# Attention fused with a soft mixture of experts: block pairs first in even steps, four pages with the first keys, at most two pages in a block, and the last values' places given back sooner

## The chip, the cores and the metric

The kernel runs on one core of one Trainium2 chip. The metric is the device time of one execution in microseconds (us); the time of a kernel is the median over several executions. Engines are named as in the profile: PE is TensorE's matrix multiply and PEld its weight load, DVE is VectorE, ACT is ScalarE, POOL is GpSimd and SP is SyncE, which here only issues transfers.

## What is computed

The reference has two stages. The first is attention for 8 batches and 8 heads with head size 64: 512 local positions, which see a window of 32 positions to each side and all 32 global keys, and 32 global positions, which see everything. The second is a soft mixture of 8 experts with 4 slots each: all 4352 rows of the attention's output are mixed into 32 slots by a softmax over the rows, each expert runs a two-layer network on its 4 slots, and each row gets its output from the slots by a softmax over the slots.

```python
k_all = np.concatenate([k_g, k_l], axis=2); v_all = np.concatenate([v_g, v_l], axis=2)
out_g = np.matmul(sm(scale * np.matmul(q_g, k_all.transpose(0, 1, 3, 2))), v_all)
s_ll = np.where(np.abs(pos[:, None] - pos[None, :]) <= 32, scale * q_l @ k_l.T, -1e9)
out_l = np.matmul(sm(np.concatenate([scale * q_l @ k_g.T, s_ll], axis=-1)), v_all)
x = concatenate([out_g, out_l], axis=2), heads side by side: rows of 512
logits = x @ phi
slot_input = softmax(logits, over rows).T @ x
slot_out[e] = np.maximum(slot_input[e] @ w1[e], 0.0) @ w2[e]
return softmax(logits, over slots) @ slot_out
```

(`sm` is a softmax with 1e-9 added to its sum; matrix shapes are shortened.) All inputs are float32. w1 and w2 together are 32 MB, q, k and v as laid out for loading some 30 MB, the output 8.9 MB.

## The kernel before, in words

**Steps.** Two heads of one batch make a step; there are 32, numbered s = 0 to 31, with batch b = s // 4, k = s % 4, and unit u = s // 2 for the global rows. The loop of line 573 runs steps 0 to 29; steps 30 and 31 and the rest are written out from line 665 on. A step holds, on PE: `scores(s)` (line 233, the 16 blocks of 32 queries against their windows of keys, 64 weight rows by 32 columns, then the masks as small products); `pv(s - 1)` (line 271, the weighted values of the step before); in odd steps `global_scores(u)` and `global_pv(u - 1)`; at k = 2 the logits of the batch before (`Dispatch.logits`, line 411), at k < 2 half of the slot sums of the batch before that (`Dispatch.sums`, line 473); in even steps transposes of x (`turn_x`, line 393) and of the global weights; and at the end `turn_exp(s)` (line 258), which transposes the shifted scores and has ACT take the exponentials. DVE takes the maxima (`top`, L251), subtracts them (`shift`, L256), divides (`norm`, L280 to L288) and keeps the running maxima and sums of the slots (L423 `Dispatch.top`, L486 `Dispatch.add`).

**pv.** It works in 16 blocks of 32 queries. 12 of them are single (32 columns of weights), and the pairs (0, 1) and (14, 15) share a window and are done with 64 columns. `GROUPS` (lines 61 and 62) lists the singles and then the two pairs; `pv` goes through it in parts of 4, 4, 4 and 2, each part for head e = 0 and then e = 1. Each float32 product is two passes on PE, so a pv is 48 passes of singles and 8 of pairs. The values stand in three tiles with shifted rows: `v` as loaded, `va` and `vb`, which POOL builds from it in `make_v` (line 195): five copies make va (L201 to L205), two make vb (L207, L208). v has 5 places (tag "v"), va 2, vb 1. A pair reads v or va, never vb; among the singles, blocks 3, 6, 9 and 12 read vb, blocks 2, 5, 8, 11 (and 13) read va.

**Loads.** All loads go through SP's queue in program order (`dma`, line 176). PE's instructions are counted in `step_count`; when the count passes a multiple of 255.22, a block begins: `pump()` (line 536) issues the block's loads, and the first of them waits for the matmul at which the block began. In a block with room for keys, pump issues one `kq` (keys and queries of a step, 592 KB) and, if a place is free, one `v` (325 KB), otherwise a page; in a block with room for a v alone, the v and a page; in any other block two pages, or three when all v are issued or when the count of pages is behind 2.5 per such block (`blocks`, `PACE`, lines 534 and 553 to 556). A page is 512 KB of w1 or w2 (`load_page`, line 499); there are 64, in the order in which the experts use them. 33 (`NWA`) have places of their own from the start.

**The tail.** After the steps, `go(n)` (line 680) issues n loads that wait for the last matmul traced: pages into own places while there are any, then whatever stands in `ready`; when ready is empty, go does nothing. The last 31 pages take places of tiles that are no longer needed: four places of kq (`borrow`, line 690), one in the area of the scores and global weights (`a2`, by the pool `wA`), six in the area of the values (`at`, by the pool `wC`), four in two places of xh (`rows_slot`, line 787), and 16 in places of pages that the first product has used (`quad`, line 910). Before the areas are free, the transposed x of the last batch (`xTm`, made in `turn_both`, line 741, and `turn_global`, line 748) is put into the five places with tag "v". Then come the logits (line 797), the slot sums, `first_product` (line 917) over pages 0 to 31, `second_product` (line 962) over pages 32 to 63 for the left half of the columns (h = 0) and for the right (h = 1), and `combine` (line 988), which makes the rows of the output from the slots and has SP store them: the left halves of the batches between the parts of the second product of h = 1, and the right halves after it.

Of the kernel before, what the change touches and what calls it, by code (L numbers as in the profile page):

```python
# [7 lines left out]
F32 = mybir.dt.float32  # L8
# [10 lines left out]
P = 128  # L19
# [39 lines left out]


SINGLE = tuple((c, 1) for c in (2, 3, 12, 13, *range(4, 12)))
GROUPS = SINGLE + ((0, 2), (14, 2))

# [12 lines left out]
def kernel(  # L76
# [194 lines left out]
    def pv(s):  # L271
        for i, j in ((0, 4), (4, 8), (8, 12), (12, 14)):
            for e in range(2):
                for c, n in GROUPS[i:j]:
                    t, qd = c // 4, c % 4
                    v, m = values(s, c)
                    q = slice(32 * qd, 32 * (qd + n))
                    mm(bV[q, t, VD * e:VD * e + VD], Ps[s][:, e, t, q], v[:, m, e, :], start=True, stop=True)
# [254 lines left out]
    free = {"kq": -1, "v": -1}  # L533
    blocks, PACE = [0], 2.5

    def pump():


        if due["kq"] < NST and due["kq"] - 4 <= free["kq"]:
            load_kq(due["kq"])  # L540
            due["kq"] += 1
            if due["v"] < NST and due["v"] - 5 <= free["v"]:
                load_v(due["v"])
                due["v"] += 1
            elif npage[0] < NWA:
                load_slot(npage[0])
        elif due["v"] < due["kq"] and due["v"] - 5 <= free["v"]:
            load_v(due["v"])
            due["v"] += 1
            if npage[0] < NWA:  # L550
                load_slot(npage[0])
        else:
            blocks[0] += 1
            for _ in range(2 + (due["v"] == NST or npage[0] + 2 < PACE * blocks[0])):
                if npage[0] < NWA:
                    load_slot(npage[0])
        gate[0] = None
# [113 lines left out]
    def pump():  # L671
# [6 lines left out]
        gate[0] = None  # L678

    def go(n):  # L680

        for _ in range(n):
            gate[0] = last[0]
            if npage[0] < NWA:
                load_slot(npage[0])
            elif ready:
                ready.pop(0)()
        gate[0] = None
# [71 lines left out]
    def both(hc, n=4):  # L760
        xTm[hc] = at.tile([P, n, NT if hc != "g" else SG], F32, tag="v", name="xTm", bufs=5)

    turns["s"] = turns["v"] = 0
    both((1, 0))
    turn_both(1, "s")
    pv(s)
    go(1)
    both("g")
    turn_global((0, 1), nc.scalar.copy)
    both((2, 0))  # L770
    turn_both(2, "s")
    d6.totals()
    both((3, 0), 2)
    both((3, 2), 2)
    norm(s)
# [4 lines left out]
    pa6 = ptile("s", 512)  # L780
    p_a2.close()
    fin = ctx.enter_context(tc.tile_pool(name="fin", bufs=1, reuse_waits="tile"))
    wA = ctx.enter_context(tc.tile_pool(name="wA", bufs=1, reuse_waits="tile"))
    new = lambda pool, tag, i: lambda: load_page(pool.tile([P, 1024], F32, tag=f"{tag}{i}", name=f"w{npage[0]}", bufs=1))
    ready.append(new(wA, "wA", 0))

# [5 lines left out]

    p_at.close()
    wC = ctx.enter_context(tc.tile_pool(name="wC", bufs=1, side="right", reuse_waits="tile"))
    ready += [new(wC, "wC", i) for i in range(NWC)]
    go(3)
    for hc in ("g", 0, 1, 2, 3):
        c = slice(P, NT) if hc == "g" else slice(0, P) if hc == 0 else slice(0, NT)
        for t in range(4):
# [6 lines left out]
            mm(pl[32 * t:32 * t + 32, c], phisb[:, 0 if hc == "g" else hc, :], x, start=(hc == "g"), stop=(hc == 3))  # L806
    go(1)
    d6.sums(pa6, 0, 512)
# [179 lines left out]
    def combine(h, b, whole=True):  # L988
# [12 lines left out]
        else:  # L1001
            os = [wC.tile([P, 4, 256], F32, tag=f"wC{b - 2}", name=f"ob{h}_{b}", bufs=1)]
        n = 4 if b < B else 2
# [125 lines left out]
```

## Time and profile before

| | us |
|---|---|
| median of 3 runs | 265.3 |
| lowest and highest run | 264.77, 267.85 |
| profiled execution, its time | 266.62 |
| its span, first to last instruction | 264.8 |
| mean granted clock of TensorE in it | 0.98 |

A line of groups gives the source line, engine, operation, the tiles as out<-in with their shapes, how often, the busy time and mean duration, and the engine's idle time ahead with what ended it. A line of waits reads: who waited <- for whom: us in total, times, longest. The view in order of time gives start, duration, engine, line, operation, tiles, shape and count; instructions of the same kind that follow each other are merged, and a shape such as 128*32 is the weight's rows and columns. "SPq" rows are transfers being issued, not their data. Line numbers are those of the kernel before, and a line can be that of a helper: L164 is every matmul, L167 every transpose and L177 every load.

### The profile page before, as it was taken

How to read it: one execution, taken by the hardware profiler on the slowest of the kernel's cores; microseconds unless marked ns; L12 is line 12 of the kernel's file. 1: busy time of each engine (PE TensorE's matmuls, PEld its weight loads, DVE VectorE, ACT ScalarE, POOL GpSimd, SP SyncE). 2: the span in 40 equal slices, each digit the busy share in tenths (PEclk: the TensorE clock that was granted, in tenths of full speed). 3: DMA queues.
4: the chain of work that ended last, by engine and by line, in shares of the span. 5: the costliest groups of instructions: out<-in, count | busy, mean ns of one | idle time of the engine just before them, and what ended most of it. 6: DMA issues, size and time to landing. Idle time of an engine off the chain costs nothing.

```text
span 264.8 us, 14386 instructions
## 1 busy us (share of the span) xinstructions
PE 244.8 (92%) x6438; PEld 177.6 (67%) x6438; DVE 174.1 (66%) x373; ACT 100.7 (38%) x225; POOL 127.2 (48%) x292
## 2 busy tenths in 40 slices
PE   8699999999999999999999999999999999999860
PEld 5578778778777777787777878777784334644430
DVE  0686677877978788777778796978775233333650
ACT  0334534434454443354544545443454003133330
POOL 0785775738685756676474738675740000000000
PEclk9799999999999999999999999999999999999995
DMA  7957587877676787868776877669699999999998
GB/s 223 321 179 244 206 259 246 256 273 233 223 237 219 243 268 254 245 244 285 230 245 231 262 271 238 213 188 336 217 368 322 386 415 411 408 408 373 341 342 286
DMA packets 27870, 73.82 MB, mean 279 GB/s; under 512 B 2464, under 2 KB 11040, under 8 KB 27808
## 3 DMA queue, kind: packets, MB, share of 16 engines
q1 hardware_dynamic: 27808, 72.90, 80.1%
q8 instruction: 50, 0.82, 1.2%
q14 instruction: 12, 0.10, 0.1%
HBM read 63.98 MB, written 8.91 MB: 275 GB/s over the span
## 4 chain that ended last, share of the span: by engine, by line
PE 73%; DVE 15%; ACT 3%; DMA 2%; issue 2%; SPq 1%; DVEq 0%; POOL 0%
PE bM L164 14%; PE bT L167 13%; PE pair L164 12%; PE bV L164 12%; PE bS L164 11%; PE one L164 4%; DVE sp L256 3%; DVE mx L251 3%; PE bV L167 3%; DMA kq<-in_kq_dram 2%; DVE xh L288 2%; PE bM L167 2%; ACT xT L408 1%; DVE ob L1009 1%; DVE lv L370 1%
## 5 line engine op out<-in xcount | busy, mean ns | idle before, releaser
L267 ACT ACTIVATE sp<-bT 128x512 f32<-128x512 f32 x64 | 34.8, 595 | 60.8 <-PE bT L167 56.8
L251 DVE TENSOR_REDUCE mx<-bS 128x8 f32<-128x1024 f32 x31 | 37.9, 1221 | 18.8 <-PE bS L164 18.6
L164 PE MATMUL bV<-va,sp 128*32 128x65 f32 (+1 forms) x768 | 41.8, 224 | 1.1 <-DVE xh L288 0.7
L256 DVE TENSOR_TENSOR sp<-bS,mx 128x1024 f32<-128x1024 f32 x31 | 38.0, 1224 | 4.8 <-PE bV L164 1.3
L164 PEld LDWEIGHTS bV<-va,sp 128*32 128x32 f32 (+1 forms) x768 | 33.6, 114 | 9.2 <-issue 7.2
L167 PE MATMUL bT<-con,sp 128*128 128x128 f32 x256 | 34.7, 279 | 2.4 <-DVE sp L256 2.4
L164 PE MATMUL bS<-kq 64*32 64x128 f32 x1984 | 36.3, 274 | 0.0
L201 POOL COPY va<-v 128x520 f32<-128x520 f32 x32 | 19.9, 622 | 33.7 <-DMA v<-in_vS_dram 30.1
L167 PEld LDWEIGHTS bT<-con,sp 128*128 128x128 f32 x256 | 28.4, 142 | 7.5 <-DVE sp L256 3.6
L164 PE MATMUL bV<-v,sp 128*32 128x65 f32 (+1 forms) x512 | 32.5, 223 | 0.4 <-issue 0.4
L164 PEld LDWEIGHTS bS<-kq 64*32 64x32 f32 x1984 | 27.7, 105 | 5.3 <-issue 5.1
L164 PE MATMUL bV<-vb,sp 128*32 128x65 f32 x512 | 28.6, 223 | 0.2 <-POOL vb L208 0.2
L164 PEld LDWEIGHTS bV<-v,sp 128*32 128x32 f32 (+1 forms) x512 | 25.7, 116 | 3.4 <-issue 0.5
L350 POOL COPY xg<-og 32x64 f32<-32x64 f32 x64 | 14.8, 231 | 25.5 <-DVE og L344 16.4
L288 DVE TENSOR_TENSOR xh<-bV,r 128x512 f32<-128x512 f32 x32 | 22.1, 691 | 3.8 <-PE bM L164 2.9
L164 PEld LDWEIGHTS bV<-vb,sp 128*32 128x32 f32 x512 | 23.2, 109 | 0.4 <-POOL vb L208 0.3
L164 PE MATMUL bM<-kq 64*32 64x128 f32 (+3 forms) x256 | 20.1, 343 | 2.8 <-DMA kq<-in_kq_dram 2.5
L207 POOL COPY vb<-v 64x520 f32<-64x520 f32 x32 | 19.7, 616 | 4.4 <-PE bV L164 2.7
L202 POOL COPY va<-v 32x520 f32<-32x520 f32 x32 | 19.6, 612 | 2.0
L208 POOL COPY vb<-v 64x520 f32<-64x520 f32 x32 | 19.6, 612 | 1.7
L1009 DVE COPY ob<-pair 128x512 f32<-128x512 f32 x19 | 12.4, 687 | 10.4 <-PE pair L164 10.3
L164 PEld LDWEIGHTS bM<-kq 128*64 128x64 f32 (+1 forms) x256 | 13.6, 141 | 6.3 <-DMA kq<-in_kq_dram 2.8
(195 smaller groups left out, 411.9 us busy)
## 6 DMA issues: line engine op xcount, KB each, us to landing
w<-in_w_dram SPq DMA_DIRECT2D x64, 512.0 KB, 6.6
kq<-in_kq_dram SPq DMA_DIRECT2D x31, 592.0 KB, 4.2
v<-in_vS_dram SPq DMA_DIRECT2D x32, 325.0 KB, 4.7
out_dram<-ob SPq DMA_DIRECT2D x14, 512.0 KB, 4.4
out_dram<-ob SPq DMA_DIRECT2D x4, 256.0 KB, 4.5
kq<-in_kq_dram SPq DMA_DIRECT2D x2, 296.0 KB, 3.1
out_dram<-ob SPq DMA_DIRECT2D x4, 128.0 KB, 3.5
mks<-in_mk_dram SPq DMA_DIRECT2D x1, 176.0 KB, 3.6
```

Of the source, the lines that this page charges most:

```text
L164: return step_count(4 if rhs.dtype == F32 else 2, nc.tensor.matmul(o, lhsT, rhs, **kw))
L167: return step_count(2, nc.tensor.transpose(o, a, i))
L201: cp(va[:, 0:4], v[:, 0:4])
L202: cp(va[0:32, 0:4], v[0:32, 1:5])
L207: cp(vb[64:128], v[64:128, 0:4])
L208: cp(vb[0:64], v[0:64, 1:5])
L251: nc.vector.reduce_max(mxs[s], bank(s).rearrange("p e t k -> p (e t) k"), axis=AX.X)
L256: nc.vector.tensor_tensor(sps[s], bank(s).rearrange("p e t k -> p (e t) k"), bc(mxs[s], P), ALU.subtract)
L267: nc.scalar.activation(Ps[s][:, e], pt, AF.Exp, scale=SCALE)
L288: nc.vector.tensor_tensor(xhs[b][:, hc].rearrange("p t (e d) -> p t e d", e=2), o[:, :, :, 0:D], bc(r, D), ALU.mult)
L350: engines[j](xgs[b // 4][p0:p0 + 32, 256 * g + D * j:256 * g + D * j + D], ogs[u][32 * j:32 * j + 32])
L1009: copies[turn[0] % 2](os[i] if not whole else os[0][:, 2 * i:2 * i + 2, :], pcs[i])
```

## The change

Four things are edited.

1. `pv` takes the pairs of blocks first when s is odd, which is the pv that runs in an even step, and last when s is even, as before. `GROUPS` becomes `SINGLE` and `PAIRS`.
2. `pump` adds a page to a block with kq and v as long as fewer than 9 kq have been issued, and a block without kq or v gets two pages, or three only when all v are issued; `blocks` and `PACE` are gone.
3. `go` remembers in `owed` what it could not issue for want of an entry in `ready` and issues it at a later go.
4. In the tail, the transposed x of head pair 1 and of the global rows share one place with tag "va" instead of two with tag "v"; the other three keep places with tag "v". The pools `a2` and `at` are closed right after pv(31). `wC` becomes six pools of one page each, opened in the reverse order, the fourth and sixth are filled first, the other four after the logits; the fifth is 1072 wide instead of 1024, of which the page uses 1024.

```diff
--- before.py
+++ after.py
@@ -58,8 +58,9 @@
 
 
 
+
 SINGLE = tuple((c, 1) for c in (2, 3, 12, 13, *range(4, 12)))
-GROUPS = SINGLE + ((0, 2), (14, 2))
+PAIRS = ((0, 2), (14, 2))
 
 
 def block_window(c):
@@ -269,9 +270,10 @@
     xhs = {}
 
     def pv(s):
-        for i, j in ((0, 4), (4, 8), (8, 12), (12, 14)):
+        parts = [SINGLE[i:i + 4] for i in range(0, 12, 4)]
+        for part in parts + [PAIRS] if s % 2 == 0 else [PAIRS] + parts:
             for e in range(2):
-                for c, n in GROUPS[i:j]:
+                for c, n in part:
                     t, qd = c // 4, c % 4
                     v, m = values(s, c)
                     q = slice(32 * qd, 32 * (qd + n))
@@ -531,7 +533,6 @@
 
     due = {"kq": 3, "v": 2}
     free = {"kq": -1, "v": -1}
-    blocks, PACE = [0], 2.5
 
     def pump():
 
@@ -539,10 +540,11 @@
         if due["kq"] < NST and due["kq"] - 4 <= free["kq"]:
             load_kq(due["kq"])
             due["kq"] += 1
-            if due["v"] < NST and due["v"] - 5 <= free["v"]:
+            v = due["v"] < NST and due["v"] - 5 <= free["v"]
+            if v:
                 load_v(due["v"])
                 due["v"] += 1
-            elif npage[0] < NWA:
+            if npage[0] < NWA and (not v or due["kq"] < 9):
                 load_slot(npage[0])
         elif due["v"] < due["kq"] and due["v"] - 5 <= free["v"]:
             load_v(due["v"])
@@ -550,8 +552,7 @@
             if npage[0] < NWA:
                 load_slot(npage[0])
         else:
-            blocks[0] += 1
-            for _ in range(2 + (due["v"] == NST or npage[0] + 2 < PACE * blocks[0])):
+            for _ in range(2 + (due["v"] == NST)):
                 if npage[0] < NWA:
                     load_slot(npage[0])
         gate[0] = None
@@ -677,13 +678,17 @@
                 ready.pop(0)()
         gate[0] = None
 
+    owed = [0]
+
     def go(n):
 
-        for _ in range(n):
+        owed[0] += n
+        while owed[0] and (npage[0] < NWA or ready):
+            owed[0] -= 1
             gate[0] = last[0]
             if npage[0] < NWA:
                 load_slot(npage[0])
-            elif ready:
+            else:
                 ready.pop(0)()
         gate[0] = None
 
@@ -758,31 +763,38 @@
                     copy(xTm[hc, t0][:, :, P:NT], p[:, t0:t1])
 
     def both(hc, n=4):
-        xTm[hc] = at.tile([P, n, NT if hc != "g" else SG], F32, tag="v", name="xTm", bufs=5)
+        xTm[hc] = at.tile([P, n, NT], F32, tag="v", name="xTm", bufs=5)
 
     turns["s"] = turns["v"] = 0
-    both((1, 0))
+    x1 = at.tile([P, 6, P], F32, tag="va", name="xT1").rearrange("p a b -> p (a b)")
+    xTm[1, 0] = x1[:, 0:4 * NT].rearrange("p (t k) -> p t k", k=NT)
+    xTm["g"] = x1[:, 4 * NT:4 * NT + P].rearrange("p (t k) -> p t k", k=SG)
+    both((2, 0))
+    both((3, 0), 2)
+    both((3, 2), 2)
     turn_both(1, "s")
     pv(s)
+    p_a2.close()
+    fin = ctx.enter_context(tc.tile_pool(name="fin", bufs=1, reuse_waits="tile"))
+    wA = ctx.enter_context(tc.tile_pool(name="wA", bufs=1, reuse_waits="tile"))
+    new = lambda pool, tag, i: lambda: load_page(pool.tile([P, 1024], F32, tag=f"{tag}{i}", name=f"w{npage[0]}", bufs=1))
+    ready.append(new(wA, "wA", 0))
+
+    p_at.close()
+    wC = [ctx.enter_context(tc.tile_pool(name=f"wC{i}", bufs=1, side="right", reuse_waits="tile"))
+          for i in reversed(range(NWC))][::-1]
+    ready += [new(wC[i], "wC", i) for i in (3, 5)]
     go(1)
-    both("g")
     turn_global((0, 1), nc.scalar.copy)
-    both((2, 0))
+    go(2)
     turn_both(2, "s")
     d6.totals()
-    both((3, 0), 2)
-    both((3, 2), 2)
     norm(s)
     turn_global((2, 3), nc.vector.tensor_copy)
     turn_both(3, "v", 0, 2)
     turn_both(3, "s", 2, 4, nc.vector.tensor_copy)
     pl = banks["m"][1][:, 0:NT]
     pa6 = ptile("s", 512)
-    p_a2.close()
-    fin = ctx.enter_context(tc.tile_pool(name="fin", bufs=1, reuse_waits="tile"))
-    wA = ctx.enter_context(tc.tile_pool(name="wA", bufs=1, reuse_waits="tile"))
-    new = lambda pool, tag, i: lambda: load_page(pool.tile([P, 1024], F32, tag=f"{tag}{i}", name=f"w{npage[0]}", bufs=1))
-    ready.append(new(wA, "wA", 0))
 
     def rows_slot():
 
@@ -790,10 +802,6 @@
         load_page(t[:, 0])
         load_page(t[:, 1])
 
-    p_at.close()
-    wC = ctx.enter_context(tc.tile_pool(name="wC", bufs=1, side="right", reuse_waits="tile"))
-    ready += [new(wC, "wC", i) for i in range(NWC)]
-    go(3)
     for hc in ("g", 0, 1, 2, 3):
         c = slice(P, NT) if hc == "g" else slice(0, P) if hc == 0 else slice(0, NT)
         for t in range(4):
@@ -804,7 +812,10 @@
             else:
                 x = xTm[hc, t // 2 * 2 if hc == 3 else 0][:, t % 2 if hc == 3 else t, :]
             mm(pl[32 * t:32 * t + 32, c], phisb[:, 0 if hc == "g" else hc, :], x, start=(hc == "g"), stop=(hc == 3))
-    go(1)
+
+    wide = lambda: load_page(wC[4].tile([P, 1072], F32, tag="wC4", name=f"w{npage[0]}", bufs=1)[:, 0:1024])
+    ready += [*(new(wC[i], "wC", i) for i in range(3)), wide]
+    go(3)
     d6.sums(pa6, 0, 512)
     go(1)
     ready.append(rows_slot)
@@ -999,7 +1010,7 @@
         elif b < 2:
             os = [kqp.tile([P, 4, 256], F32, tag="kq", name=f"ob{h}_{b}", bufs=4)]
         else:
-            os = [wC.tile([P, 4, 256], F32, tag=f"wC{b - 2}", name=f"ob{h}_{b}", bufs=1)]
+            os = [wC[b - 2].tile([P, 4, 256], F32, tag=f"wC{b - 2}", name=f"ob{h}_{b}", bufs=1)]
         n = 4 if b < B else 2
         pcs = [ptile("c", 2, 512)[:, :, 0:256] for _ in range(n // 2)]
         for t in range(n):
```

## The prediction

> **What bounds the kernel now.** I read the page first, for the engines' shares and the chain of work that ended last; then the table by stretches, to split the attention steps (up to about 196 us) from the experts' stage; then TensorE's own waits in these two parts.
>
> ```profile
> PE 244.8 (92%) x6438; PEld 177.6 (67%) x6438; DVE 174.1 (66%) x373; ACT 100.7 (38%) x225; POOL 127.2 (48%) x292
> ...
> PE 73%; DVE 15%; ACT 3%; DMA 2%; issue 2%; SPq 1%; DVEq 0%; POOL 0%
> ```
>
> In the next view the columns behind each stretch are the busy times of PE, PEld, DVE, ACT and POOL, the granted clock, DMA's share and its GB/s.
>
> ```profile
> 10.00:20.00 10.00, 9.58 (x263) 7.71 (x248) 7.49 (x11) 3.66 (x7) 8.11 (x17) 0.90 0.65 205
> 20.00:40.00 20.00, 19.38 (x659) 15.59 (x659) 13.34 (x25) 8.44 (x16) 13.83 (x33) 1.00 0.75 239
> 40.00:60.00 20.00, 19.99 (x601) 16.16 (x600) 15.53 (x32) 8.19 (x19) 11.34 (x26) 1.00 0.76 253
> 196.00:206.00 10.00, 9.60 (x200) 5.78 (x188) 5.17 (x22) 3.76 (x12) 1.05 (x5) 1.00 0.94 349
> 206.00:216.00 10.00, 9.77 (x94) 3.32 (x90) 3.11 (x11) 0.00 (x0) 0.00 (x0) 1.00 1.02 404
> ```
>
> TensorE carries 73% of the chain and is busy nearly all of every stretch; DMA is busy three quarters of the time in the steps and without a pause in the experts' stage (1.02). So the steps are TensorE's, while two suspects stand in the experts' stage. The waits tell them apart. From 6 to 196 us TensorE's list holds one transfer, at the start, and from 196 us to the end none; the longest rows of the two lists:
>
> ```profile
> PE bM L164 <- DMA kq<-in_kq_dram: 2.5, 1, 2.5
> PE bT L167 <- DVE sp L256: 2.4, 6, 0.7
> ```
>
> ```profile
> PE pair L164 <- ACT sa L981: 0.5, 1, 0.5
> ```
>
> No matmul of the experts waits for a page. What ends last are the outputs, which need the experts' last products; SP issues the last four from 256.23 us:
>
> ```profile
> 184.55 45.38 SPq L177 DMA_DIRECT2D w<-in_w_dram  x36
> ...
> 256.23 3.49 SPq L1014 DMA_DIRECT2D out_dram<-ob  x4
> ```
>
> The 36 pages are issued over 45.38 us, 1.26 us each: my price of a page where DMA is full. The end is set by TensorE's chain to the last products, plus the output drain behind it.
>
> **Part 1, pairs of blocks first in even steps.** pv(s - 1) runs in step s, so the order changes for odd s - 1: in even steps, in pv(29) of the tail and in pv(31). No matmul is added; what changes is which shapes are neighbours. TensorE's order of time around pv(15), in step 16 (start, duration; the shape is weight rows*columns):
>
> ```profile
> 98.00 0.42 PE L164 MATMUL bS<-mks 64*32 64x384 bf16 x8
> 98.35 0.24 PE L164 MATMUL bV<-va,sp 128*32 128x65 f32 x1
> ...
> 98.97 0.22 PE L164 MATMUL bV<-vb,sp 128*32 128x65 f32 x1
> 99.01 0.22 PE L164 MATMUL bV<-v,sp 128*32 128x65 f32 x1
> ...
> 99.03 0.22 PE L164 MATMUL bV<-vb,sp 128*32 128x65 f32 x1
> 99.18 0.27 PE L164 MATMUL bV<-v,sp 128*64 128x65 f32 x1
> ...
> 99.41 0.22 PE L164 MATMUL bV<-va,sp 128*64 128x65 f32 x1
> 99.56 0.64 PE L164 MATMUL bM<-xh,d 128*32 128x256 f32 x8
> 100.13 0.66 PE L167 MATMUL bT<-con,xh 128*128 128x128 f32 x4
> ```
>
> From the last single (99.03) to the first pair (99.18) it is 0.15 us, from the last pair (99.41) to the first sum (99.56) again 0.15; where the shape stays 128*32, four more start 0.04 after the last of the four before (98.97 to 99.01). A change of shape costs 0.11 beyond that cadence. Now there are four changes in such a step: masks to singles, singles to pairs, pairs to sums (or logits), these to transposes. Pairs first leave three: masks to pairs, pairs to singles, and behind the singles' sums the transposes. That saves 0.11. The sums also start up quicker: after a change they take 0.57 (99.56 to 100.13), without one, in the next step, 0.55:
>
> ```profile
> 106.58 0.62 PE L164 MATMUL bM<-xh,d 128*32 128x256 f32 x8
> 107.13 0.44 PE L167 MATMUL bT<-con,sp 128*128 128x128 f32 x2
> ```
>
> That makes 0.13 us in each even step with sums or logits right behind pv: by the code steps 6 to 28 (logits at k = 2 from b = 1, sums at k = 0 from b = 2), 12 steps. In steps 2 and 4, in step 30 and after pv(31) transposes follow, and the number of changes stays. In odd steps pairs stay last, ahead of the 128*64 global scores: nothing changes.
>
> Does VectorE let the saving through? Its subtraction for the next transposes ends at 101.06 in step 16, and they begin at 101.17, so there at most 0.11 can reach TensorE; I take half, 0.05, for this step and for one more like it.
>
> ```profile
> 99.83 1.23 DVE L256 TENSOR_TENSOR sp<-bS,mx 128x1024 f32<-128x1024 f32 x1
> ```
>
> ```profile
> 101.17 0.28 PE L167 MATMUL bT<-con,sp 128*128 128x128 f32 x1
> ```
>
> But VectorE itself idles in even steps for ScalarE's xT copy, which comes from transposes right behind pv and the sums; its list of waits:
>
> ```profile
> DVE acc L486 <- ACT xT L408: 5.4, 6, 1.8
> DVE bm L423 <- ACT xT L408: 4.4, 4, 1.6
> ```
>
> So VectorE's work for the odd step behind it moves up with TensorE, and the rest passes: 10 x 0.13 + 2 x 0.05 = 1.4 us.
>
> Unseen is masks straight to pairs (64*32 to 128*64). Every change above starts the next matmul 0.07 before the end of the one ahead (98.00 + 0.42 against 98.35, 99.03 + 0.22 against 99.18, 99.41 + 0.22 against 99.56, 99.56 + 0.64 against 100.13), whatever the shapes; so I take masks to pairs like masks to singles, no difference. The bounds are a change that is free, 0.11 less, and one that costs double, 0.11 more: 1.5 us either way over the 14 pv's behind masks (steps 4 to 30). The Trainium skill (TensorEngine Tiling (Array Packing), Key Properties) says that a change of tiling mode drains TensorE; by that rule it costs what is in flight, the masks in both orders, and the sum stays; no row here shows this pair of modes.
>
> **Part 1b, late values.** Pairs need v and va, not vb, so pairs first postpone the first read of vb by 0.23 for the pairs (99.18 to 99.41) and 0.15 for the change: 0.38 us. Twice vb was late, in pv(9) and pv(25):
>
> ```profile
> 61.87 0.30 PE L164 MATMUL bV<-va,sp 128*32 128x65 f32 x2
> 62.13 0.25 PE L164 MATMUL bV<-vb,sp 128*32 128x65 f32 x2
> ```
>
> ```profile
> 160.16 0.30 PE L164 MATMUL bV<-va,sp 128*32 128x65 f32 x2
> 160.61 0.25 PE L164 MATMUL bV<-vb,sp 128*32 128x65 f32 x2 [0.15 <-POOL vb L208]
> ```
>
> The stalls are 0.26 and 0.45 us. The first is covered whole; of the second 0.38 is, and part 2 should take the other 0.07. I count 0.7. In return pv gives vb back up to 0.4 us later in even steps. POOL is behind five va copies then; should it come early, POOL would wait 0.4, and TensorE only if vb were the last to be ready.
>
> **Part 2, the page rhythm.** I ran the rule of pump() by hand with the counts of the code. kq and v keep blocks and order. The first blocks of kq3, kq4, kq6 and kq7 get a page each: four more by step 5. The blocks of three in steps 15, 19, 23 and 29 become blocks of two: four fewer. Before step 30's first block both versions have issued 28 pages, which the trace confirms for the kernel before (64 less the 36 above). So this brings nothing into the tail earlier. Four pages cost 4 x 1.26 = 5.0 us of DMA early, where the stretches above leave 0.35 x 10 + 0.25 x 20 + 0.24 x 20 = 13.3 idle. On SP a page is one more issue behind v; the next kq and v in the queue wait for their own block anyway. The bounds are 0 and one page, 1.26 us, of delay to the v that is already latest, v9 in pv(9); I take 0.
>
> The block of three in step 23 is the one that hurt: v25 was issued behind it, POOL waited 3.99 us for it, and vb came late in pv(25).
>
> ```profile
> 145.22 2.39 SPq L177 DMA_DIRECT2D w<-in_w_dram  x3
> ...
> 150.06 0.38 SPq L177 DMA_DIRECT2D v<-in_vS_dram  x1
> ```
>
> ```profile
> 156.77 0.62 POOL L201 COPY va<-v 128x520 f32<-128x520 f32 x1 [3.99 <-DMA v<-in_vS_dram]
> ```
>
> A page less ahead of v25 is up to 1.26 us; 0.07 of it is needed.
>
> **Part 3, places of the last values.** The last batch's transposed x moves from five "v" places to three and one "va" place, the pools close before norm(31), and pages go into the new places sooner: two after pv(31), one after the next transposes, four behind the logits; go() remembers what it could not issue. Compute order is the same. SP's new wait is for pv(31) to leave sp. All later pages queue behind it, and matmuls use those only in the second product, after all 32 pages of the first. What the stream can gain is DMA's idle share here, 0.06 of the 10 us from 196: 0.6 us. Since no expert matmul waits for a page, I count 0 at the end; if that cover were gone, 0.6.
>
> **Sum.** The profiled execution has a span of 264.8 us in a time of 266.62, 1.8 around it. 264.8 - 1.4 - 0.7 = 262.7, with 1.8 264.5. That execution lies 1.3 above the median of the runs, 265.3; on the median it is 265.3 - 2.1 = **263.2 us**.
>
> **Rivals.** (a) *DMA sets the end.* The full stretch speaks for it, the waits without a page against it. Then part 3 adds its 0.6: 262.6. The Trainium skill (Perfetto Trace Analysis, Identifying the Most-Contended Engine) will not take matmul busy time as TensorE's measure and looks at weight loads; they fill 3.32 of 10 us at 206 to 216, beside a full DMA, so by that rule the stage is DMA's and this rival's time holds. (b) *VectorE absorbs the saved changes.* For it: six waits of TensorE for sp. Against: VectorE's waits for xT. Only the 0.7 is left: 264.6. (c) *Early pages push v9.* It lands 1.26 later and pv(9) waits 0.26 + 1.26 - 0.38 = 1.1, where I forecast none: 264.3. (d) *Slower: masks to pairs is dear.* Place: the 14 pv's behind masks. It decides from 2.1 / 14 = 0.15 on top of masks to singles, more than a whole change (0.11), against the four changes that all look alike; at 0.25 it is 14 x 0.25 = 3.5 less the 2.1: 266.7. (e) *The change doesn't do what it says*: the stalls move and the changes of shape cost what they did, 265.3.
>
> **How the numbers follow.** Forecast 0.53, (a) 0.13, (b) 0.14, (c) 0.08, (d) 0.06, (e) 0.04, something unseen and faster 0.02. The likeliest's own range is 261.7 to 264.7, by the masks' bounds of 1.5. All cases but (d) lie in 261.7 to 265.3; the runs of one kernel here go from 264.77 to 267.85, so I take 261.3 to 265.9, which leaves (d) and the unseen out. Two per cent is 5.3 us, about what a measurement of this kernel can tell from no change: below 260.0 only the unseen (0.02) comes, above 270.6 only (d) well beyond its price (0.02).
>
> **What would show it.** Right: pv to sums 0.04 apart in steps 6 to 28; masks to first pair like masks to first single now, 0.35 from the first mask; no wait for vb in pv(9) and pv(25); 28 pages before step 30; TensorE's end 2 us earlier with the drain behind it as long as now. Wrong: masks to pairs 0.15 dearer, new waits for vb in steps 5 to 10, pages in TensorE's waits after 206 us, or an end that moves without TensorE's.

## The result, and the profile after

The changed kernel is slower by about 1%: 268.6 us median of 6 runs (268.07 to 271.26) against 266.48 us of the kernel before (264.77 to 272.06, 6 runs), a ratio of 1.0106 with a 95% interval of 1.0059 to 1.0152. On another chip (e9_after_again below) it was 1.0066 (1.0028 to 1.0104). The forecast was 2 us less. The profiled execution took 268.07 us with a span of 266.3; the one of before 266.62 with 264.8. Line numbers are one higher than before ahead of `pv` and more behind it. Ratios leave out executions more than 1.5% above a kernel's fastest, and the profiled executions of e1_pairs, e6_no_early and e13_pairs_pump are such, so of them only the ratios are used, and one list of stalls.

Busy time and the chain of waits that ended last, from the page of the changed kernel:

```profile
PE 242.6 (91%) x6438; PEld 176.4 (66%) x6438; DVE 174.7 (66%) x373; ACT 100.4 (38%) x225; POOL 126.8 (48%) x292
...
PE 74%; DVE 14%; issue 3%; ACT 2%; DMA 2%; SPq 1%; DVEq 1%
```

TensorE is busy 2.2 us less than before, and "issue", time in which it waits for nothing that the profile shows, has grown from 2% to 3% of the chain. The same five stretches as before (busy PE, PEld, DVE, ACT, POOL, granted clock, DMA's share, GB/s):

```profile
10.00:20.00 10.00, 8.81 (x255) 7.03 (x254) 6.77 (x11) 4.17 (x9) 7.79 (x16) 1.00 0.80 272
20.00:40.00 20.00, 17.31 (x589) 13.78 (x569) 12.57 (x23) 7.67 (x14) 13.63 (x33) 1.00 0.90 303
40.00:60.00 20.00, 20.00 (x644) 16.22 (x640) 15.60 (x30) 7.96 (x18) 11.54 (x26) 1.00 0.76 244
196.00:206.00 10.00, 9.57 (x208) 5.97 (x208) 5.28 (x21) 4.20 (x13) 1.40 (x6) 1.00 1.01 393
206.00:216.00 10.00, 9.77 (x92) 3.41 (x95) 2.79 (x10) 0.00 (x0) 0.00 (x0) 1.00 1.03 413
```

From 20 to 40 us DMA is at 0.90 where it was at 0.75, and TensorE is busy 17.31 us where it was 19.38: 2 us are lost where the early pages load. TensorE's waits from 6 to 196 us:

```profile
PE bT L168 <- DVE sp L257: 3.0, 6, 0.9
PE bS L165 <- issue: 2.7, 2, 1.9
PE bM L165 <- DMA kq<-in_kq_dram: 1.7, 1, 1.7
```

The longest wait with no releaser before was 0.4 us; now one of 1.9 us stands there. In TensorE's order of time it is in step 6, between two halves of the same mask products, which have the same operands:

```profile
37.52 0.40 PE L165 MATMUL bS<-mks 64*32 64x384 bf16 x4
39.85 0.34 PE L165 MATMUL bS<-mks 64*32 64x384 bf16 x4 [1.93 <-issue]
```

What was on its way in that time is seen in SP's list, in which the third row is three pages in two blocks, one of them the early page beside kq7 and v6:

```profile
31.08 0.33 SPq L178 DMA_DIRECT2D kq<-in_kq_dram  x1
31.50 1.16 SPq L178 DMA_DIRECT2D v<-in_vS_dram  x1
32.72 2.91 SPq L178 DMA_DIRECT2D w<-in_w_dram  x3
```

And the queues show a passenger that the prediction did not look at. The page's third part has 50 transfers of 16 KB on a queue of their own, named instruction: the engines' code, loaded while the kernel runs.

```profile
q1 hardware_dynamic: 27808, 72.90, 79.3%
q8 instruction: 50, 0.82, 1.2%
```

In the steps one comes every 4 us or so. Between 32.4 and 37.5 us, 5.1 us, there is none, with the engines 92% full of loads (packets, MB, share):

```profile
q1 hardware_dynamic: 428, 1.46, 92.2%
q14 instruction: 1, 0.01, 0.4%
```

In the kernel before, the stretch with the same loads of kq7 and v6, from 31.6 to 36.4 us, is 62% full and has one such transfer at its beginning; the next one starts at 36.52:

```profile
q1 hardware_dynamic: 284, 0.94, 61.7%
q8 instruction: 1, 0.02, 1.8%
```

In the changed kernel it comes in the next stretch, from 37.5 to 38.6 us: one packet, 5.6% of 16 engines for 1.1 us, that is 0.99 us long.

```profile
q8 instruction: 1, 0.02, 5.6%
```

The trace has it from 37.58 to 38.57, and TensorE goes on 1.28 us later, at 39.85. This is a rule and not a single case: in both kernels every idle time of TensorE of 0.12 us or more between 9 and 206 us for which the profile names no releaser ends 1.2 to 1.9 us after the end of a q8 transfer. Over the fourteen profiles of the table further down it holds for 93 of 95 such times, where by chance about one in six would fall into these 0.7 us (the transfers in the steps are 4.3 us apart on average). I call these stalls *late code*. That q8 carries TensorE's own code is inferred: its 6438 products and 6438 weight loads over 50 transfers are 257 instructions a transfer, and the kernel's blocks of loads are 255.22 counted instructions long, so code and loads come nearly in step. Late code comes to 1.4 us in the kernel before and 4.3 in the changed one; between 30 and 45 us alone to 0.26 and 2.34.

The other loss is behind the last product. TensorE's last products are copied out 0.6 us later than before, but the end is 1.45 later. The last two copies, of before and then of the changed kernel:

```profile
255.90 1.29 DVE L1009 COPY ob<-pair 128x512 f32<-128x512 f32 x2 [0.80 <-PE pair L164]
```

```profile
256.49 1.29 DVE L1020 COPY ob<-pair 128x512 f32<-128x512 f32 x2 [0.80 <-PE pair L165]
```

From the end of these (257.18 and 257.78) to the end of the span it is 7.6 us and 8.5 us. I call this the drain. The rate at which outputs leave, in a stretch ahead of it and one in it, again before and then after:

```profile
253.18:255.18 2.00, 2.00 (x18) 1.10 (x18) 1.29 (x2) 1.16 (x3) 0.00 (x0) 1.00 1.08 383
258.18:261.18 3.00, 0.00 (x0) 0.00 (x0) 0.00 (x0) 0.00 (x0) 0.00 (x0) 0.50 1.09 385
```

```profile
253.78:255.78 2.00, 2.00 (x18) 1.05 (x17) 1.29 (x2) 1.16 (x3) 0.00 (x0) 1.00 1.01 343
258.78:261.78 3.00, 0.00 (x0) 0.00 (x0) 0.00 (x0) 0.00 (x0) 0.00 (x0) 0.78 1.03 348
```

DMA is full in all four, yet it moves 383 and 385 GB/s before and 343 and 348 after. These outputs are mostly the right halves of batches 2 to 7, which leave from the wC places that part 3 moved.

The difference between the two profiled executions adds up so: the changed one was 1.05 us ahead at step 4 (its first keys came sooner, which is not of the change); step 6 turns this into 0.90 behind; the rest of the steps and the experts win 0.30 back; the drain loses 0.85: 1.45 in all.

### The profile page after: what moved, and what is told of

It reads as the page before. It is cut to its first block, busy times and chain, and to the rows that moved or that the text cites. A ratio compares the mean times of both kernels' runs of the same rounds, so it can differ in the third digit from the quotient of the medians.

```text
span 266.3 us, 14383 instructions
## 1 busy us (share of the span) xinstructions
PE 242.6 (91%) x6438; PEld 176.4 (66%) x6438; DVE 174.7 (66%) x373; ACT 100.4 (38%) x225; POOL 126.8 (48%) x292
## 4 chain that ended last, share of the span: by engine, by line
PE 74%; DVE 14%; issue 3%; ACT 2%; DMA 2%; SPq 1%; DVEq 1%
PE bT L168 14%; PE bM L165 13%; PE bS L165 12%; PE pair L165 12%; PE bV L165 12%; PE one L165 4%; DVE sp L257 3%; DVE mx L252 3%; PE bV L168 3%; PE bM L168 2%; DMA kq<-in_kq_dram 2%; DVE xh L290 2%; DVE ob L1020 1%; ACT xT L410 1%; DVE cm L370 1%
## 5 line engine op out<-in xcount | busy, mean ns | idle before, releaser
L165 PE MATMUL bV<-v,sp 128*32 128x65 f32 (+1 forms) x512 | 34.1, 224 | 0.6 <-ACT sp L268 0.4
L165 PE MATMUL bM<-kq 64*32 64x128 f32 (+3 forms) x256 | 19.2, 308 | 2.1 <-DMA kq<-in_kq_dram 1.7
L165 PEld LDWEIGHTS bM<-kq 128*64 128x64 f32 (+1 forms) x256 | 13.0, 129 | 5.5 <-DMA kq<-in_kq_dram 2.1
```

What stands on the lines that cost most here:

```text
L165: return step_count(4 if rhs.dtype == F32 else 2, nc.tensor.matmul(o, lhsT, rhs, **kw))
```

## The experiments

The theory: part 1 gives what was forecast; the early pages of part 2 stand in front of TensorE's code and make it late; part 3 puts the outputs in places that are read more slowly. Rivals: the pairs cost elsewhere; part 2 is neutral; the drain is long because of the order of transfers; the stalls come by chance.

### The parts alone

e1_pairs: the kernel before with the edit of `pv` alone.

```diff
-        for i, j in ((0, 4), (4, 8), (8, 12), (12, 14)):
+        parts = [SINGLE[i:i + 4] for i in range(0, 12, 4)]
+        for part in parts + [PAIRS] if s % 2 == 0 else [PAIRS] + parts:
             for e in range(2):
-                for c, n in GROUPS[i:j]:
+                for c, n in part:
```

> The kernel before with part 1 alone: pairs first in even steps. Theory of late code: the change as a whole came out slower because TensorE stands still in the middle of products that wait for nothing the profile shows, each time shortly after the end of a 16 KB transfer of the queue q8 instruction, and the early pages delay these transfers. It expects here what part 1 and 1b of the prediction priced, 2.1 us less than the kernel before (ratio 0.992), pv(9) and pv(25) without their stalls, and no stall of over 1 us in step 6. Rival, the pairs cost elsewhere: VectorE's small operations in steps 22 and 23 (0.4 us later there in the changed kernel) and pv(31) (0.18 longer) come from the new order; then this kernel gains at most 1.0 us (ratio 0.996 or more).

Measured: 0.9917 (0.9873 to 0.9961), 2.2 us less, which is what was forecast for the pairs and more than the 1.0 us that the rival allowed. The size is less sure than the interval says: only six of the twelve runs enter the ratio, and the medians of all runs, 267.29 us against 267.10 of the kernel before beside them, show no gain. e11_pairs_tail_wide below, which has the pairs too, is 1.8 us less than the kernel before.

e2_pump: the kernel before with the edit of `pump` alone.

```diff
-            elif npage[0] < NWA:
+            if npage[0] < NWA and (not v or due["kq"] < 9):
...
-            for _ in range(2 + (due["v"] == NST or npage[0] + 2 < PACE * blocks[0])):
+            for _ in range(2 + (due["v"] == NST)):
```

> The kernel before with part 2 alone: four early pages, never three in a block. Theory of late code: slower by 2 to 3.5 us (ratio 1.008 to 1.013), with TensorE idle for about 2 us without a releaser between 33 and 42 us, after a q8 instruction transfer that started 5 us or more behind the one before. Rival, part 2 is neutral as forecast: within 0.7 us of the kernel before, the stall of 0.45 us in pv(25) gone.

Measured: 1.0060 (1.0023 to 1.0098), 1.6 us more: slower, by somewhat less than expected. TensorE's order of time from 30 to 45 us has the loss in two pieces, at the same two places of the program as in the changed kernel:

```profile
34.48 0.87 PE L164 MATMUL bM<-kq 128*64 128x256 f32 x8 [1.17 <-issue]
39.30 0.34 PE L164 MATMUL bS<-mks 64*32 64x384 bf16 x4 [0.55 <-issue]
```

e3_tail: the kernel before with part 3 alone (go, the places of xTm, the pools; the diff of the change from go on).

> The kernel before with part 3 alone: places of the last values given back sooner, wC in six pools. Theory of late code: no change (ratio 0.998 to 1.002). Rival, the drain: the outputs of the last batches leave from new places and their packets of 1024 bytes take 48 to 50 ns where they took 46 to 47; then the last product ends as before and the end is 0.9 us later (ratio 1.003).

Measured: 1.0010 (0.9974 to 1.0046). The ratio can't tell 0 from 0.9 us, but the drain can: 8.3 us, where e2_pump had 7.8. So the long drain comes with part 3.

e4_pairs_tail: the changed kernel with the old page rhythm.

```diff
-            if npage[0] < NWA and (not v or due["kq"] < 9):
+            elif npage[0] < NWA:
...
-            for _ in range(2 + (due["v"] == NST)):
+            blocks[0] += 1
+            for _ in range(2 + (due["v"] == NST or npage[0] + 2 < PACE * blocks[0])):
```

> The changed kernel with the page rhythm of the kernel before, so parts 1 and 3 without part 2. Theory of late code: 2.1 us faster than the kernel before (ratio 0.992), like the pairs alone. Rival drain: 1.2 us faster (0.9955), 0.9 lost after the last product. Rival pairs cost elsewhere: no faster than 1.0 us (0.996).

Measured: 1.0009 (0.9971 to 1.0048), slower than any of the three said, with a drain of 8.3 and only 0.8 us of late code in the profiled execution. By itself this was a riddle; e11_pairs_tail_wide below takes it up again.

e13_pairs_pump: the kernel before with the edits of e1_pairs and e2_pump, without part 3.

> Parts 1 and 2 without part 3. If the parts add up: 0.6 us less than the kernel before (ratio 0.995 to 1.000). If pairs and page rhythm make each other worse, so that the steps' saving runs into later code and nothing is gained: ratio 1.002 to 1.007. In both the drain is that of the old places, 7.6 to 7.8 us.

Measured: 1.0015 (0.9973 to 1.0056), between the two. The saving of the pairs doesn't show beside the new page rhythm; whether the two add up (-0.6 us) or make each other worse (+0.5 and more) stays open.

### Which pages make the code late

e6_no_early: the changed kernel without early pages.

```diff
-            if npage[0] < NWA and (not v or due["kq"] < 9):
+            if npage[0] < NWA and not v:
```

> The changed kernel without the four early pages: never more than two pages in a block, none beside a kq and a v; so four pages more are left for the tail. Theory of late code: no stall of over 0.6 us between 33 and 42 us, where the changed kernel has 0.41 and 1.93; about 2 us faster than the changed kernel, ratio to the kernel before 1.000 to 1.004. Rival, the early pages are not what delays the code: the stall of about 2 us in step 6 stays and the ratio too, 1.01.

Measured: 1.0023 (0.9990 to 1.0055), and from 30 to 45 us one stall of 0.26. That is as the theory has it, though the interval overlaps the one of the changed kernel in e9_after_again (1.0028 to 1.0104).

e10_early2_wide: early pages only beside kq3 and kq4, and the fifth wC place 1088 wide.

```diff
-            if npage[0] < NWA and (not v or due["kq"] < 9):
+            if npage[0] < NWA and (not v or due["kq"] < 6):
...
-    wide = lambda: load_page(wC[4].tile([P, 1072], ...
+    wide = lambda: load_page(wC[4].tile([P, 1088], ...
```

> The changed kernel with early pages only beside the first two later loads of keys (kq3 and kq4) instead of four, and the fifth wC place 1088 wide. Theory of late code: the pages beside kq6 and kq7, with the two pages behind them, are what pushes the code of step 6; without them no stall of over 0.6 us between 33 and 42 us, and with the places right a drain of 7.5: faster than the kernel before by 1 us or more (ratio 0.996 or less). Rival, any page added beside keys and values costs: ratio 0.998 to 1.005, with a stall of 1 us or more before 42 us.

Measured: 264.87 us median (262.71 to 270.93) against 267.58, ratio 0.9906 (0.9864 to 0.9949): this beats both kernels. No stall at all between 30 and 45 us, drain 7.5.

e14_late2_wide: the same number of pages, but beside kq6 and kq7.

```diff
-            if npage[0] < NWA and (not v or due["kq"] < 6):
+            if npage[0] < NWA and (not v or due["kq"] in (7, 8)):
```

> The changed kernel with the fifth wC place 1088 wide and early pages only beside kq6 and kq7, where the fast variant had them only beside kq3 and kq4; the same number of pages. Theory of late code, with the burst in steps 4 and 5 as the cause: stalls of 1 us or more together between 33 and 42 us, ratio 0.998 to 1.005. Rival, two pages are harmless wherever they are, only four are too many: ratio 0.989 to 0.994 as with kq3 and kq4, no such stall.

Measured: 1.0012 (0.9969 to 1.0056), with the stalls back at both places (TensorE's order of time, 30 to 45 us):

```profile
33.44 0.87 PE L165 MATMUL bM<-kq 128*64 128x256 f32 x8 [0.40 <-issue]
39.36 0.34 PE L165 MATMUL bS<-mks 64*32 64x384 bf16 x4 [1.65 <-issue]
```

So it is not how many pages come early but where. Behind kq7 follow the two pages of the next block, and kq6, v5, kq7, v6 and four pages are issued within 9.5 us. Late code between 30 and 45 us separates the profiles of the table further down: 1.7 to 2.3 us in the five with pages beside kq6 and kq7 (the changed kernel, e2, e5, e9, e14), 0 to 0.85 in the nine without.

### The place of the loads against the code

e7_phase: the kernel before with its blocks begun half a block sooner. Nothing is loaded more or less.

```diff
-    BLOCK, AHEAD, PRE = 255.22, -24, 63
+    BLOCK, AHEAD, PRE = 255.22, 104, 63
```

> The kernel before with the blocks of loads begun 128 counted instructions (half a block, some 2 us) sooner, the rest as it was. Theory of late code: in the kernel before a block's loads are issued within 0.6 us of the q8 instruction transfer of that block, so that code is ahead of them and behind data that is 4 us old; now it comes behind loads that are only 2 us old, starts over 1 us later against TensorE's place in the program in many blocks, and TensorE's idle time without a releaser, each 1.0 to 2.0 us behind the end of such a transfer, grows from 1.4 us to over 6 us: slower by 5 us or more (ratio 1.02 or more). Rival, these stalls belong to places of the program or come by chance: sum of 1 to 4 us as in the others, ratio within 0.5% of 1.

Measured: 292.04 us, ratio 1.0874 (1.0805 to 1.0943), 23 us slower. TensorE's waits without a releaser from 9 to 206 us, with the longest in its order of time:

```profile
PE bM L164 <- issue: 10.9, 9, 3.8
PE bV L164 <- issue: 4.4, 6, 1.4
PE bS L164 <- issue: 4.0, 5, 1.7
```

```profile
98.67 0.66 PE L164 MATMUL bM<-xT,phisb 128*32 128x128 f32 x8 [3.82 <-issue]
```

They come to 19.3 us where the kernel before has 1.4, and all but 0.3 of them end 1.2 to 1.9 us behind a q8 transfer; the wait at 98.67 is behind one that ran from 96.40 to 97.29. That is the bulk of the 23 us. The program's places did not change, so the stalls are not bound to them.

e12_pairs_later: e1_pairs with the blocks begun 0.5 us later (AHEAD of -56).

> Part 1 alone, with the blocks of loads begun 32 counted instructions (some 0.5 us) later. Theory of late code: the code's transfer is asked for near the beginning of a block and now comes ahead of the block's own data more often, so the sum of the stalls behind q8 instruction transfers falls to 1.5 us or less (the pairs alone had 4.1, the kernel before 1.4), and the time is that of the pairs alone or up to 2 us less (ratio 0.985 to 0.992). Rival, the stalls come by chance whatever the place of the block within 0.5 us: sum 2 to 4 us, ratio 0.992 or, with keys and values 0.5 us later, above.

Measured: 1.0151 (1.0089 to 1.0213), 6 us slower than e1_pairs. The waits without a releaser, 9 to 206 us:

```profile
PE bS L164 <- issue: 2.7, 4, 1.3
PE bV L164 <- issue: 2.6, 2, 2.2
PE bM L164 <- issue: 2.0, 4, 0.7
```

They come to 7.3 us instead of the expected 1.5. Late keys or values do not explain it: TensorE's list has no wait for a transfer in these 197 us, and 0.4 us for va. My expectation was wrong in sign: later is not better, so "asked for near the beginning of a block" is too simple a picture. What holds is that half a microsecond in the phase between loads and code moved the time by more than every term of the prediction: by 6 us against e1_pairs, and the kernel is 4 us slower than the one before, pairs and all.

### The places of the outputs

The built programs give each place an address: in the kernel before wC0 to wC5 start 256 bytes behind a multiple of 512; in the changed kernel, where the fifth is 1072 wide, wC0 to wC4 start 64 bytes behind one and wC5 256; the page places and the one kq place from which outputs leave start 96 behind in both.

e5_wide: the changed kernel with 1088 instead of 1072, so that wC0 to wC4 start at a multiple of 512.

> The changed kernel with the fifth of the wC places 1088 wide instead of 1072, which moves wC0 to wC4 by 64 bytes: they start at a multiple of 512 bytes, where with 1072 they start 64 bytes behind one, and in the kernel before 256 bytes behind one. Theory of places: the outputs that leave from such places are read more slowly when these do not start at a multiple of 256 bytes (0.345 MB per us with packets of 1024 bytes of 47 to 49 ns, against 0.385 and 46.0); it expects from the last copy of an output to the end 7.6 to 7.8 us, where the changed kernel has 8.5 and the two other kernels with part 3 have 8.3, and 0.6 us less of the whole. Rival, the earlier pages and the order of transfers in the tail make the drain long: 8.3 to 8.5 as before. Stalls for late code as in the changed kernel, as nothing moves in the steps.

Measured: drain 7.5 us, ratio 1.0008 (0.9969 to 1.0046). The same two stretches:

```profile
253.83:255.83 2.00, 2.00 (x18) 1.05 (x17) 1.29 (x2) 1.16 (x3) 0.00 (x0) 1.00 1.09 385
258.83:261.83 3.00, 0.00 (x0) 0.00 (x0) 0.00 (x0) 0.00 (x0) 0.00 (x0) 0.50 1.09 385
```

385 GB/s again, with the order of transfers as in the changed kernel: it was the places. The ratio is lower than those of the changed kernel by more than the 0.6 us expected (2.6 and 1.6 us); its interval overlaps that of e9_after_again, so how much of this is more than the drain is open. Late code stays, 1.8 us between 30 and 45 us.

e8_pairs_pad: e1_pairs with 160 bytes ahead of all places of pages.

```diff
     wrm = keep.tile([P, P], BF16, name="wrm")
+    keep.tile([P, 40], F32, name="pad")
```

> The kernel before with part 1 alone, and 160 bytes of padding ahead of the pages' places, so that pages, kq and all outputs start 256 bytes behind a multiple of 512 instead of 96. Theory of places: the outputs that leave from kq and page places (now 0.345 to 0.355 MB per us) come up to 0.385, and the drain shrinks from 7.8 to 7.3 us or less; 0.5 us on top of the pairs' 2.1, ratio 0.990. Rival: the place makes no difference, drain 7.6 to 7.8 us and ratio 0.992 as with the pairs alone.

Measured: drain 7.4 us, ratio 0.9956 (0.9915 to 0.9998). The drain shrank by less than was expected, and the ratio, with 4.1 us of late code in the profiled execution (2.5 of it at 131 us), can't be told from that of e1_pairs.

e11_pairs_tail_wide: e4_pairs_tail with 1088.

> Parts 1 and 3 with the page rhythm of before and the fifth wC place 1088 wide. If part 3 costs only through the places, this is as fast as the pairs alone, 2.2 us less than the kernel before (ratio 0.990 to 0.994), with a drain of 7.5 us where the same kernel with 1072 had 8.3. If part 3 costs elsewhere too, 0.996 or more.

Measured: 0.9933 (0.9886 to 0.9979), drain 7.8 where 7.5 was expected. With the places mended, no cost of part 3 beside the pairs is to be seen. (The step from e4_pairs_tail is 2 us, of which the drain explains 0.5; the intervals overlap.)

e15_early2_wide_pad: e10_early2_wide with the 160 bytes.

> The fastest variant so far (early pages beside kq3 and kq4, fifth wC place 1088 wide) with 160 bytes of padding ahead of the pages' places, so that every output leaves from a place at a multiple of 256 bytes. Theory of places: a drain of 7.2 us or less where it was 7.5, ratio 0.988 to 0.991. Rival, places no longer matter as the last outputs are right already: drain 7.5, ratio 0.9906 or, by chance of the stalls, above.

Measured: drain 7.1 us, ratio 0.9924 (0.9881 to 0.9967): the drain as expected, the total no better than e10_early2_wide, with 2.1 us of late code between 12 and 28 us of the profiled execution.

### The change once more

> The changed kernel once more, beside the three below. If its parts add up as the runs of the parts alone say (pairs 2.2 us less, page rhythm 1.6 more, tail 0.3 to 0.9 more) it is within 0.5 us of the kernel before (ratio 0.998 to 1.002). If the parts make each other worse, it stays at 1.008 to 1.013. In both cases the stalls for late code come to over 2 us between 9 and 62 us and the drain takes 8.2 to 8.5.

Measured (e9_after_again): 268.78 us, ratio 1.0066 (1.0028 to 1.0104), 1.8 us more; late code of 2.1 us between 30 and 45 us, drain 8.5. The ratio lies between the two that were said, nearer to the parts making each other worse, and does not decide. All profiles but the three named at the beginning, in one table:

| kernel | early pages | ratio | late code, 9 to 206 us | of it 30 to 45 us | drain, us |
|---|---|---|---|---|---|
| before | none | 1 | 1.4 | 0.3 | 7.6 |
| after | four | 1.0106 | 4.3 | 2.3 | 8.5 |
| e9, after again | four | 1.0066 | 4.6 | 2.1 | 8.5 |
| e2, pump | four | 1.0060 | 3.7 | 1.7 | 7.8 |
| e5, 1088 | four | 1.0008 | 3.9 | 1.8 | 7.5 |
| e14, 1088 | at kq6, kq7 | 1.0012 | 3.1 | 2.1 | 7.7 |
| e10, 1088 | at kq3, kq4 | 0.9906 | 1.3 | 0 | 7.5 |
| e15, 1088, pad | at kq3, kq4 | 0.9924 | 3.5 | 0.1 | 7.1 |
| e3, tail | none | 1.0010 | 2.7 | 0 | 8.3 |
| e4, pairs, tail | none | 1.0009 | 0.8 | 0 | 8.3 |
| e11, pairs, 1088 | none | 0.9933 | 1.7 | 0.4 | 7.8 |
| e8, pairs, pad | none | 0.9956 | 4.1 | 0 | 7.4 |
| e12, 0.5 us later | none | 1.0151 | 7.3 | 0.7 | 7.5 |
| e7, half a block | none | 1.0874 | 19.3 | 0.8 | 7.5 |

The table also shows what an execution's chance is: outside 30 to 45 us late code varies by 2 us between kernels that don't differ there. One profile's total is no evidence for a difference of that size; the ratios and the place are.

## Why the prediction was wrong, step by step

**Part 1 was right in its rows; its total is less sure.** Pairs are neighbours of the masks now, in step 16 of the changed kernel:

```profile
99.03 0.42 PE L165 MATMUL bS<-mks 64*32 64x384 bf16 x8
99.39 0.27 PE L165 MATMUL bV<-v,sp 128*64 128x65 f32 x1
...
99.62 0.39 PE L165 MATMUL bV<-va,sp 128*64 128x65 f32 x2
99.77 0.25 PE L165 MATMUL bV<-vb,sp 128*32 128x65 f32 x2
...
100.44 0.22 PE L165 MATMUL bV<-vb,sp 128*32 128x65 f32 x1
100.48 0.61 PE L165 MATMUL bM<-xh,d 128*32 128x256 f32 x8
101.02 0.66 PE L168 MATMUL bT<-con,xh 128*128 128x128 f32 x4
```

Masks to pairs take 0.36 from the first mask, like masks to singles (0.35); from the last single to the first sum it is 0.04 instead of 0.15; from the first product to the transposes 1.63 us instead of 1.78. That is 0.15 in this step where 0.13 was priced. Rival (d), masks to pairs are dear, falls by the same rows.

**Part 1b was right.** vb is no longer waited for; in pv(25) it follows the pairs without a gap (its row has no bracket), and v25, now behind two pages and not three, holds POOL up 3.01 us instead of 3.99:

```profile
161.56 0.25 PE L165 MATMUL bV<-vb,sp 128*32 128x65 f32 x2
```

```profile
156.95 0.61 POOL L202 COPY va<-v 128x520 f32<-128x520 f32 x1 [3.01 <-DMA v<-in_vS_dram]
```

Both parts together are worth 2.2 us by the ratio of e1_pairs, against 2.1 in the sum, with the doubt said there. In the profile of the changed kernel the gain is not all to be seen: TensorE's waits for sp grew from 2.4 to 3.0 us and its late code from 62 us on by 0.35. The remaining 0.8 or so I could not place.

**Part 2 is the step that failed.** The count was right: as before, 36 pages are left at step 30's first block (185.01 us). The cost was not. "The bounds are 0 and one page, 1.26 us, of delay to the v that is already latest ...; I take 0." It measured +1.6 us (e2_pump), and the early pages beside kq6 and kq7 do it (e10 against e14). Two things were wrong in it. The idle share of DMA over 10 or 20 us (13.3 us in all) said nothing about the moment: the harm is done within a few us, in blocks in which loads were already queued. And the list of those who wait behind a page was incomplete: I looked for the next kq and v, rival (c) let v9 be late, but the one that was late was the code. The profile of before had the hint in lines that I quoted or read past: "issue 2%" in the chain, and the q8 row of part 3 of the page. The 1.4 us of late code in the kernel before were there to be set beside the 50 transfers.

How the delay comes about stays open. In the changed kernel the transfer at 37.58 us starts 6.2 us after the one before it, with the engines 92% full between the two. That alone is not the cause: the kernel before has a gap as long, from 93.17 to 99.35 us, and no stall behind it. The Trainium skill (DMA: Bandwidth & Descriptors, Queues, rings and completion order) has each DMA engine take turns between queues, packet by packet; by that rule code on a queue of its own would wait for a packet and not for a backlog. When a transfer was asked for is not in the trace, so no run here shows where in the way it waits, or whether the rule holds for it.

**Part 3 failed by what it left out.** As forecast the last page lands sooner (238.47 us against 239.71), the stretch from 196 us is filled (1.01 against 0.94), and the end gains nothing. But the drain, "as long as now" in the prediction, is 0.85 us longer, since the fifth place is 192 bytes wider than a page and five places begin 64 bytes off. The rows of before name no addresses. The Trainium skill says (DMA: Bandwidth & Descriptors, How a descriptor splits into AXI transactions) that a descriptor, one run of bytes of a transfer, is cut into pieces of 256 bytes, and that one which does not start at a multiple of 256 bytes also fetches the unused bytes ahead of its start. By it, an estimate, with the trace's packets of 1024 bytes taken as descriptors: 1024 bytes from 64 behind take 34 beats of 32 bytes in five pieces instead of 32 in four. The runs agree in the direction, and that 0 and 256 bytes behind a multiple of 512 are equally good (385 GB/s in both); the measured price, 385 against 343 and 348 GB/s, is 11 to 12% more time for a byte, between the 6% of the beats and the 25% of the pieces.

**The sum.** Pairs -2.2, page rhythm +1.6, drain +0.85 make +0.25 us; measured were +1.8 and +2.8. Each of these ratios is uncertain by about 1 us, so chance can make this gap. It may also lie in the -2.2, the least sure of the three (e1_pairs), or in pairs that gain less beside the other parts (e4_pairs_tail, e13_pairs_pump); that stays open. Of the 5.4 us from the forecast of 263.2 to the measured 268.6, 1.2 are the base: the sum starts from 265.3, the median of three runs, and that of six is 266.48. The range, 261.3 to 265.9, was too narrow for a simple reason: it held the bounds of the costs that were listed, and late code and the longer drain were on no list.

## What to carry to other kernels

When loads are moved, ask what else uses the DMA engines: if the page shows a queue named instruction, set its transfers beside the engine's waits for "issue", and judge a load by what is in flight at its moment, not by the idle share of its stretch. When a buffer's place is moved or padded, look at where it starts: keep the source of an output at a multiple of 256 bytes. And of a change with several parts, measure each alone before giving it up; here two early pages instead of four and 16 more columns of padding turned 1% slower into 1% faster.

## What the runs showed of the hardware that was not expected

TensorE stands still when its code comes late, and the profile names no releaser for it: 19.3 us in one kernel whose loads were only begun half a block sooner, all but 0.3 us of it in stalls that end 1.2 to 1.9 us behind the end of a 16 KB transfer of 0.9 to 1.4 us. With the blocks half a microsecond later, the kernel with the pairs was 4 us slower than the one before. And a full DMA moved outputs in pieces of 1024 bytes at 383 to 385 GB/s from places at 0 or 256 bytes behind a multiple of 512, at 343 to 348 from places 64 behind.
